# Loads run two units ahead in place of three from the tenth prepared unit on rather than from the twelfth

## The chip, the cores and the metric

One core of a Trainium2 chip. The metric is device time in microseconds (us) of one execution; medians over repeated executions are given with their range. "Clock" is the granted clock of TensorE: the share of its full rate that the throttle let through, 1.0 being all of it.

In the profile rows SPq is SyncE's queue, PE is TensorE, DVE VectorE and POOL GpSimd. A row gives start and duration in us, the line of kernel.py, the operation, what it writes and reads, and how many instructions are merged in it; a bracket gives the idle time before it and what ended it.

## The reference, cut to what matters

```python
B, H, S, D = 4, 8, 768, 64                # q, k, v in float32
for b in range(nb):                       # linear attention with decay, block by block
    intra = einsum(q_b, k_b) * Dmask;  intra = einsum(intra, v_b)
    inter = einsum(q_b * lam_pow, kv_state)
    out[b] = intra + inter
    kv_state = lam_block * kv_state + einsum(k_b * rev_pow, v_b)
x = out.transpose(0, 2, 1, 3).reshape(3072, 512)
return ((x @ w_a) * (x @ w_b)) @ w_out    # 512 -> 1536 -> 512
```

The kernel works on 24 units of 128 tokens (six for each of four batch entries). A unit needs its q, k and v, 256 KB each.

## The kernel before

Units are gathered into eight groups (4, 1, 2, 4, 4, 4, 4, 1) for the feed-forward product. While TensorE works on one group, the attention pieces of the next units are put between its matmuls at fixed slots. `used` counts prepared units; a load is put on SyncE's queue only if it is not too far ahead of it.

```python
LOOKAHEAD = (3, 2)
DMA_T_FROM = 9
...
PLAN = { ...
    2: [(0, "V", 6), (1, "T", 7), (1, "P", 8), (4, "T", 8), (4, "P", 9), (6, "S", 7),
        (6, "S", 8), (7, "V", 7), (6, "P", 10), (10, "V", 8),
        (12, "Q", (7, 8, 9, 10)), (12, "P", 11), (13, "V", 9), (14, "P", 12),
        (14, "O2", (9, 10))],
    3: [(3, "S", 11), (3, "S", 12)], ...
...
ld_pool = ctx.enter_context(tc.tile_pool(name="ld", bufs=4))   # per q, k and v
...
def load_x(w, u):
    ...
    nc.sync.dma_start(out=t, in_={"q": qr, "k": kr, "v": vr}[w][b, nb])
...
def pump():
    while pending:
        kind, c = pending[0]
        if kind in "abo":
            if len(staged) >= W_BUFS:
                return
        elif c >= used["u"] + LOOKAHEAD[used["u"] > 11]:
            return
        pending.pop(0)
        ...                                    # load_w or load_x
...
def prep_k(u):
    make_ks(u, "dve" if u < n0 + 2 else "pool")
    make_qs(u, "pool")
    used["u"] = u + 1
    if u >= DMA_T_FROM:                        # q and k transposed by a DMA, SBUF to SBUF
        qkT = qkT_pool.tile([128, 2, HP, 128], BF16, name="qkT", tag="qkT")
        nc.sync.dma_start_transpose(out=..., in_=U[u]["qk"]...)
...
def prep_v(u):
    make_vb(u, "pool" if u < n0 + 3 else "dve")
    pump()
...
def pieces_O(us, nxt=()):                      # "Q": outputs of us, scores of nxt
    kqs = [score_banks() for u in nxt]
    for u in us:
        inter(u)
    for u, kq in zip(nxt, kqs):
        scores(u, kq)                          # needs qkT of u
    for u in us:
        intra(u)
        ...
```

"P" of a unit is prep_k and then prep_v: scale k and q (GpSimd), put the transpose on SyncE's queue, cast v (VectorE), then pump the loads. So transposes and loads share one queue, in the order in which the program emits them. Below, L12 stands for unit 12's three loads and T10 for unit 10's transpose.

Of the kernel before, what the change touches and what calls it, by code (L numbers as in the profile page):

```python
# [30 lines left out]
LOOKAHEAD = (3, 2)  # L31
# [33 lines left out]
def kernel(  # L65
# [59 lines left out]
    def load_x(w, u):  # L125
        b, nb = divmod(u, NB)
        t = ld_pool.tile([128, H, D], F32, name=w + "f", tag=w + "f")
        nc.sync.dma_start(out=t, in_={"q": qr, "k": kr, "v": vr}[w][b, nb])
        raw[u, w] = t
# [10 lines left out]
    def load_w(kind, c):  # L140
        t = wst_pool.tile([128, 1024], F32, name="wst", tag="wst")
        if kind == "o":
            t = t[:].rearrange("p (k n) -> p k n", k=2)
            nc.sync.dma_start(out=t, in_=wo_r[:, 2 * c:2 * c + 2, :])
        else:
            w = W_CHUNKS[c]
            t = t[:, :KS * w].rearrange("p (k n) -> p k n", k=KS)
            r = wa_r if kind == "a" else wb_r
            nc.sync.dma_start(out=t, in_=r[:, :, w_off[c]:w_off[c + 1]])
        staged[kind, c] = t  # L150

    def cast_w(kind, c, eng):
        t = staged.pop((kind, c))
        if kind == "o":
            dst = wo_sb[:, 2 * c:2 * c + 2, :]
        else:
            dst = (wa_sb if kind == "a" else wb_sb)[:, :, w_off[c]:w_off[c + 1]]
        if eng == "act":
            nc.scalar.copy(dst, t)
        elif eng == "pool":  # L160
            nc.gpsimd.tensor_copy(dst[:, :, :128], t[:, :, :128])
            nc.gpsimd.tensor_copy(dst[:, :, 128:], t[:, :, 128:])  # L162
        else:
            nc.vector.tensor_copy(dst, t)
        pump()
# [9 lines left out]
    used = {"u": 0}  # L175
# [4 lines that stand above are left out]
            if kind in "abo":  # L180
                if len(staged) >= W_BUFS:
                    return
            elif c >= used["u"] + LOOKAHEAD[used["u"] > 11]:
                return
            pending.pop(0)
            if kind in "abo":
                load_w(kind, c)
            else:
                load_x(kind, c)
# [23 lines left out]
    for u in range(n0):  # L213
        load_x("v", u)
    pump()


# [69 lines left out]
# [3 lines that stand above are left out]
# [416 lines left out]
```

## Time and profile before

| | before |
|---|---|
| time, median (range) | 234.9 us (234.56 to 235.3, 5 runs) |
| profiled execution: time, span, granted clock | 235.62 us, 233.9 us, 1.0 |
| TensorE busy | 225.5 us (96%) |
| TensorE's waits behind the start-up | one, 1.49 us |
| TensorE asks for T10's result / has it | 77.56 / 79.05 us |

The profiled execution was a slow one, 0.7 us above the median and above all five runs quoted.

### The profile page before, as it was taken

Reading aid. Unit: us, or ns where it says so; the run is one execution under the profiler, and the core shown is the slowest. Engines: PE = TensorE matmul, PEld = TensorE weight load, DVE = VectorE, ACT = ScalarE, POOL = GpSimd, SP = SyncE. Lnnn points to the kernel's source line nnn. Section 1 sums busy time; section 2 is a strip of 40 time slices with the busy share of each in tenths; the row PEclk is TensorE's granted clock in tenths of the full one; section 3 lists DMA queues with packets and bytes.
Section 4 is the critical chain, followed back from the end, with each engine's and each line's share of the span. In section 5 each row is a group of like instructions: output and inputs, shape, how many; then the busy total and the mean of one; then the engine's idle time right before and its main releaser. Section 6 shows DMA issues by size and latency. Waiting matters only on the chain.

```text
span 233.9 us, 4520 instructions
## 1 busy us (share of the span) xinstructions
PE 225.5 (96%) x1775; PEld 124.7 (53%) x1775; DVE 118.3 (51%) x204; ACT 91.1 (39%) x172; POOL 50.6 (22%) x65
## 2 busy tenths in 40 slices
PE   7799999999999799999999999999999999999993
PEld 2474444459688454454544454544454544444493
DVE  0896557536579536775235574235583323332050
ACT  3585753066363243342243342333332333332261
POOL 6070000237463333553000543001200000000000
PEclk9999999999999999999999999999999999999999
DMA  4999999999999999998659997229300220000311
GB/s 154 301 286 350 349 366 288 295 191 224 198 229 174 207 220 203 213 193 162 234 198 215 211 178 134 90 90 207 67 3 0 90 92 0 1 0 23 114 45 48
DMA packets 96389, 38.84 MB, mean 166 GB/s; under 512 B 83312, under 2 KB 91888, under 8 KB 96368
## 3 DMA queue, kind: packets, MB, share of 16 engines
q1 hardware_dynamic: 96224, 38.54, 73.3%
q8 instruction: 14, 0.23, 0.4%
q14 instruction: 7, 0.06, 0.1%
q10 hardware_dynamic: 144, 0.00, 0.0%
HBM read 28.32 MB, written 6.29 MB: 148 GB/s over the span
## 4 chain that ended last, share of the span: by engine, by line
PE 90%; DMA 5%; ACT 1%; SPq 1%; issue 0%; DVE 0%
PE a_ps L435 27%; PE b_ps L435 26%; PE op L467 26%; DMA k<-in_k_dram 3%; PE o_ps L352 3%; PE kq L310 2%; DMA qkT<-qk 2%; PE o_ps L342 2%; PE kvd L366 1%; PE tps L296 1%; ACT o_kept L458 1%; SPq L209 1%; PE kq L578 1%; ACT xT L359 0%; PE kv L366 0%; PE tk L542 0%
## 5 line engine op out<-in xcount | busy, mean ns | idle before, releaser
L447 DVE TENSOR_TENSOR ab<-a_sb,b_ps 128x512 bf16<-128x512 bf16 (+2 forms) x96 | 52.5, 553 | 76.7 <-PE b_ps L435 56.7
L435 PE MATMUL a_ps<-xT,wa_sb 128*128 128x512 bf16 (+2 forms) x384 | 77.2, 326 | 0.6 <-ACT xT L359 0.6
L435 PE MATMUL b_ps<-xT,wb_sb 128*128 128x512 bf16 (+2 forms) x384 | 77.3, 326 | 0.0
L442 ACT CAST a_sb<-a_ps 128x512 bf16<-128x512 f32 (+2 forms) x96 | 45.6, 481 | 63.2 <-PE a_ps L435 61.6
L467 PE MATMUL op<-wo_sb,ab 128*128 128x512 bf16 (+2 forms) x312 | 65.6, 363 | 0.0
L435 PEld LDWEIGHTS <-wb_sb 128*128 128x128 bf16 x384 | 34.5, 98 | 28.6
L435 PEld LDWEIGHTS <-wa_sb 128*128 128x128 bf16 x384 | 33.7, 98 | 29.0 <-POOL wa_sb L162 0.6
L467 PEld LDWEIGHTS <-ab 128*128 128x128 bf16 x312 | 28.8, 98 | 29.9
L327 DVE TENSOR_TENSOR m<-kq,lotri 128x512 bf16<-128x512 f32 x47 | 29.4, 684 | 19.3 <-PE kq L310 19.0
L259 POOL TENSOR_TENSOR qk<-kf,lp_k 128x512 bf16<-128x512 f32 x18 | 19.0, 1057 | 76.4 <-DMA kf<-in_k_dram 69.8
L264 POOL TENSOR_TENSOR qk<-qf,lp_q 128x512 bf16<-128x512 f32 x20 | 21.7, 1087 | 23.4 <-DMA qf<-in_q_dram 23.4
L462 ACT COPY o_sb<-op 128x512 f32<-128x512 f32 (+2 forms) x19 | 10.3, 541 | 34.0 <-PE op L467 34.0
L359 ACT CAST xT<-o_ps 128x512 bf16<-128x512 f32 x22 | 12.0, 590 | 19.6 <-PE o_ps L352 19.2
L398 DVE TENSOR_TENSOR st<-kvd,bdiag 128x512 bf16<-128x512 f32 x18 | 12.3, 685 | 4.7 <-PE kvd L366 3.6
L273 DVE CAST vb<-vf 128x512 bf16<-128x512 f32 x17 | 11.3, 667 | 0.0
L298 ACT COPY qkT<-tps 128x1024 bf16<-128x1024 bf16 x5 | 5.1, 1012 | 9.9 <-PE tps L296 9.9
L197 PE MATMUL idle<-idle_sb 128*128 128x128 bf16 (+1 forms) x31 | 7.5, 384 | 1.3 <-DVE idle_sb L192 1.3
L310 PE MATMUL kq<-qkT 64*128 64x128 bf16 x160 | 6.7, 218 | 1.5 <-DMA qkT<-qk 1.5
L352 PE MATMUL o_ps<-m,vb 128*64 128x128 bf16 x192 | 7.9, 222 | 0.0
L273 POOL CAST vb<-vf 128x512 bf16<-128x512 f32 x7 | 4.7, 674 | 13.9 <-DMA vf<-in_v_dram 13.9
L342 PEld LDWEIGHTS <-st 128*128 128x128 bf16 x80 | 5.4, 98 | 2.8
L352 PEld LDWEIGHTS <-vb 128*64 128x64 bf16 x192 | 5.8, 109 | 1.4
(57 smaller groups left out, 87.4 us busy)
## 6 DMA issues: line engine op xcount, KB each, us to landing
vf<-in_v_dram SPq DMA_DIRECT2D x24, 256.0 KB, 5.1
qf<-in_q_dram SPq DMA_DIRECT2D x20, 256.0 KB, 4.5
kf<-in_k_dram SPq DMA_DIRECT2D x20, 256.0 KB, 4.8
out_dram<-o_sb SPq DMA_DIRECT2D x16, 256.0 KB, 2.0
wst<-in_moe_w_a_dram SPq DMA_DIRECT2D x6, 512.0 KB, 8.7
wst<-in_moe_w_b_dram SPq DMA_DIRECT2D x6, 512.0 KB, 8.8
wst<-in_moe_w_out_dram SPq DMA_DIRECT2D x6, 512.0 KB, 8.5
out_dram<-o_kept SPq DMA_DIRECT2D x7, 256.0 KB, 2.5
```

The source lines that it names most:

```text
L259: eng_of(eng).tensor_mul(qk[:, 1], raw.pop((u, "k")), lp_k[:, u % NB].to_broadcast([128, H, D]))
L264: eng_of(eng).tensor_mul(U[u]["qk"][:, 0], raw.pop((u, "q")), lp_q[:, u % NB].to_broadcast([128, H, D]))
L273: eng_of(eng).tensor_copy(vb, vf)
L310: nc.tensor.matmul(kq[i][:, hp, :], lhsT=d["kT"][p, hp, :], rhs=d["qT"][p, hp, :], start=True, stop=True, skip_group_check=True)
L327: nc.vector.tensor_mul(m, kq[i], lotri_bc)
L352: nc.tensor.matmul(d["o"][p, hp, :], lhsT=d["vb"][:, 2 * hp + i, :], rhs=d["m"](i, hp), start=(first and hp == 0), stop=True, skip_group_c ...
L359: nc.scalar.copy(xT[:, :, col:col + BLK], o_ps)
L398: nc.vector.tensor_mul(st[:].rearrange("p hp i d -> p hp (i d)"), ps[:].rearrange("p hp i d -> p hp (i d)"), bdiag_bc)
L435: nc.tensor.matmul(ps[:, :gt], lhsT=w_sb[:, s, f * 128:(f + 1) * 128], rhs=xT[:, s, :gt], start=(s == 0), stop=(s == KS - 1))
L442: nc.scalar.copy(a_sb[:, :gt], ps[:, :gt])
L447: nc.vector.tensor_mul(ab[:, f, :gt], a_sb[:, :gt], ps[:, :gt])
L467: nc.tensor.matmul(op[:, lo:hi], lhsT=ab[:, f, t * 128:(t + 1) * 128], rhs=wo_sb[:, f, lo:hi], start=(f == 0), stop=(f == FC - 1))
```

## The change

Its intent is to change from which unit on the loads run only two units ahead. One threshold moves:

```diff
-            elif c >= used["u"] + LOOKAHEAD[used["u"] > 11]:
+            elif c >= used["u"] + LOOKAHEAD[used["u"] > 9]:
```

## The prediction

> **What bounds the kernel now.** I first read the page's busy shares and the chain that ended last. TensorE is busy 96% of the span and the chain is nine tenths matmul, so time can only come out of TensorE's few gaps, or be lost by opening new ones.
>
> ```profile
> PE 225.5 (96%) x1775; PEld 124.7 (53%) x1775; DVE 118.3 (51%) x204; ACT 91.1 (39%) x172; POOL 50.6 (22%) x65
> PE 90%; DMA 5%; ACT 1%; SPq 1%; issue 0%; DVE 0%
> ```
>
> The DMA's 5% is what a change of loads could touch. Read in order of time, the chain has two DMA pieces: the first K load (7.92 us, at the start, not touched) and one transposing DMA in the middle. The second table of waits, TensorE's alone from 62.6 us to 231 us, has a single row: waited for, total us, times, longest.
>
> ```profile
> PE kq L310 <- DMA qkT<-qk: 1.5, 1, 1.5
> ```
>
> After 85 us the same view is empty. So the only TensorE wait behind the start-up is this one. The timeline of TensorE shows where it lies, in the third group (units 7 and 8):
>
> ```profile
> 77.16 0.40 PE L310 MATMUL kq<-qkT 64*128 64x128 bf16 x8
> 79.05 0.40 PE L310 MATMUL kq<-qkT 64*128 64x128 bf16 x8 [1.49 <-DMA qkT<-qk]
> 79.38 0.64 PE L352 MATMUL o_ps<-m,vb 128*64 128x128 bf16 x16
> ```
>
> By the plan this is slot 12, "Q" of units 7, 8, 9, 10: the first eight matmuls are the scores of unit 9, the second eight those of unit 10. Unit 10's transposed q and k are late. The chain in order of time says how late:
>
> ```profile
> 73.98 0.02 SPq L282
> ...
> 74.12 4.89 DMA qkT<-qk
> 79.01 0.05 issue
> 79.05 0.40 PE kq L310 x8
> ```
>
> Issued at 74.12, landed at 79.01. To find why it was issued so late I put the two engines that precede it side by side: SyncE's queue (first fence) and GpSimd (second). Transposes start at unit 9, so the one at 68.06 is unit 9's, the one at 74.12 unit 10's; between them are the three loads of unit 12, after them those of unit 13.
>
> ```profile
> 66.64 1.25 SPq L128 DMA_DIRECT2D vf<-in_v_dram  x1
> 68.06 2.21 SPq L282 DMA_TRANSPOSE qkT<-qk  x1
> 70.33 0.56 SPq L128 DMA_DIRECT2D qf<-in_q_dram  x1
> 70.94 1.66 SPq L128 DMA_DIRECT2D kf<-in_k_dram  x1
> 72.71 0.83 SPq L128 DMA_DIRECT2D vf<-in_v_dram  x1
> 74.12 1.86 SPq L282 DMA_TRANSPOSE qkT<-qk  x1
> 76.04 0.57 SPq L128 DMA_DIRECT2D qf<-in_q_dram  x1
> 76.67 1.07 SPq L128 DMA_DIRECT2D kf<-in_k_dram  x1
> 77.83 0.86 SPq L128 DMA_DIRECT2D vf<-in_v_dram  x1
> 78.81 3.70 SPq L282 DMA_TRANSPOSE qkT<-qk  x2
> ```
> ```profile
> 67.12 1.04 POOL L259 TENSOR_TENSOR qk<-kf,lp_k 128x512 bf16<-128x512 f32 x1 [1.28 <-DMA kf<-in_k_dram]
> 68.12 1.04 POOL L264 TENSOR_TENSOR qk<-qf,lp_q 128x512 bf16<-128x512 f32 x1
> 70.70 1.04 POOL L259 TENSOR_TENSOR qk<-kf,lp_k 128x512 bf16<-128x512 f32 x1 [1.54 <-PE kq L310]
> ```
>
> GpSimd scales K of units 0 to 3 not at all and of 4 and 5 not (VectorE does), so counting its L259 rows from unit 6 the pair at 67.12 and 68.12 is unit 10. Its data were ready at 68.12 + 1.04 = 69.16; the transpose went out at 74.12, 4.96 us later. In that time SyncE was issuing: unit 9's transpose until 70.27, then unit 12's loads until 73.54. One queue issues in program order, so the loads of unit 12 stand in front of the transpose that TensorE needs next.
>
> **What the Trainium skill says.** "Perfetto Trace Analysis", section "What 'DMA-bound' means", names an issuing sequencer whose track is solid DMA slices as a bound of its own; that is SyncE here from 66.64 on. The same page, "Per-instruction lifecycle", section "DMA Instruction — HWDGE", has the profiled slice begin when semaphores are satisfied and end when descriptors are generated, the movement itself not being in it. The trace agrees: slices last 0.56 to 2.21 us in the fence above, while loads land a median 4.5 to 5.1 us after issue and transposes 4.2 us (3.0 to 5.9). "DMA: Bandwidth & Descriptors", section "Issuing engines are not separate DMA queues", has all DMAs share the same 16 engines, so removing loads from in front of a transpose also removes their traffic: the mean DMA share from 70.00 to 77.56 us is 1.42, over full by overlapping packets.
>
> **The change part by part.** No operation is added or removed; instruction counts should be equal. Loads of a unit c go out while c < used + lookahead, after prep(u) has set used = u + 1 and put unit u's transpose on the queue. Before: after prep 9, used = 10, lookahead 3: unit 12; after prep 10: unit 13; after prep 11, lookahead 2, 12 + 2 = 14: nothing; after prep 12: unit 14. Changed: after prep 9, 10 + 2 = 12: nothing; after prep 10: unit 12; after prep 11: unit 13; after prep 12: unit 14. So exactly two triples move on the queue, each behind one transpose more:
> before T9, L12, T10, L13, T11, T12, L14; changed T9, T10, L12, T11, L13, T12, L14. All from L14 on is in the same order.
>
> Step 1, T10. It waits for GpSimd (69.16) and for SyncE to finish T9 (70.27), so it goes out near 70.3 instead of 74.1, 3.8 us earlier. With the 4.89 us it took, it lands near 75.2; with the slowest of all, 5.9, at 76.2. TensorE asks for it at 79.05 - 1.49 = 77.56. The wait of 1.49 us goes, with 1.4 to 2.4 us to spare.
>
> Step 2, L12 and T11. L12 follows T10: 70.3 + 1.9 = 72.2, against 70.33, so 1.9 us later, ending near 75.4. T11's data were ready at 70.70 + 2.04 = 72.74, so T11 at about 75.5 (before 78.81).
>
> Step 3, L13. From about 77.5 against 76.04, 1.5 later.
>
> Step 4, T12. Unit 12's K was issued at 70.94 and used by GpSimd from 76.48, 5.54 later; now 72.9 + 5.5 = 78.4, plus two GpSimd ops (2.04) = 80.5. Before, T12 was the second of the pair at 78.81, at 81.27. About 0.8 us earlier despite the later load, since L13 no longer holds up T11.
>
> Step 5, T13, T14. L14 near 81.8 (before 82.56). Unit 13's K, 77.5 + 0.6 + 5 = 83, plus 2.04 = 85.1 (T13 was at 85.94). T14 was at 90.45; near 89.7 now. The scores of 11 and 12 come at 92.32, those of 13 and 14 at 100.11; after a gain of 1.5 us at 90.8 and 98.6. T12 lands by 80.5 + 5.9 = 86.4, T14 by 95.6. Both in time.
>
> Step 6, VectorE. It casts V in program order, so a late V would hold up what follows. Unit 12's V now goes out near 74.3 (before 72.71); with the median 5.1 us it is there at 79.4. VectorE reached that cast at 82.29 and would reach it near 81.2.
>
> Step 7, what gives some back. Behind the wait, VectorE has unit 9's and 10's masks (four of 0.68 us), a cast of 0.42 and unit 9's state (0.69), which unit 10's first output matmuls need. Before, masks were broken by 0.60 us of waiting; now they run through from 77.59 to about 80.2, the cast to 80.6, the state to 81.3. TensorE wants it at 82.78 - 1.49 + 0.2 = 81.5. Level, with the casts on this engine ranging from 0.42 to 1.20 us: I take off 0 to 0.5 us, 0.15 in the mean.
>
> Sum: 1.49 - 0.15 = about 1.35 us of 233.9, all of it passed on, since no wait for anything follows up to the end. 234.9 - 1.35 = 233.55, say 233.6 us.
>
> **Rivals.**
> - *T10 is not held by the loads.* The chain puts a TensorE matmul (a_ps, ending 73.94) ahead of T10's semaphore instruction, and 0.58 us pass between 73.54 and 74.12. If that were a true dependency, T10 would stay and the time be 234.9. Against it: that matmul is at slot 10 or so, and T10 is emitted at slot 6; a DMA cannot wait for a later instruction of the program. The buffer it overwrites was last read by unit 6's scores, before 62 us. I take the name for a coincidence of two events (1 in 15).
> - *The wait only moves* to unit 9's state, or to PSUM banks whose masks are read later relative to TensorE: a gain of 0.5 to 1.0, so 234.0 to 234.4 (1 in 6).
> - *The shorter lookahead starves units 12 and 13.* For it: GpSimd already sits 3.74 us waiting for unit 12's K and 3.10 for unit 13's. Against: at 5.5 us per load the chain above still leads the need by 3 to 4 us, and VectorE's V cast by 1.8. A slow landing (the V loads reach 8.6 us) would cost TensorE 1 to 2 us: 235 to 236 (1 in 20).
>
> **Range and chances.** Full gain 233.2 to 233.8 with the before's scatter of about 0.3 either way; moved wait up to 234.4; null 234.9. Hence 232.9 to 234.6 for 8 in 10. Two per cent is 4.7 us, three times the only wait in reach; nothing of that size is in the trace in either direction, so within 2% has 0.97.
>
> **What would show it.** Right: SyncE's queue shows two transposes in a row near 68 and 70.3; the 1.49 us row is gone; the third group's end and all behind it lie about 1.4 us earlier; counts are equal. Step 1 is wrong if unit 10's transpose still starts near 74 or lands after 77.6; steps 4 to 6 are wrong if a new TensorE wait stands before the scores at 92 or 100, or VectorE waits on a V load near 81; step 7 is mis-sized if a wait above 0.3 us appears before the output matmuls near 81.3.

## The result, and the profile after

| | before | after |
|---|---|---|
| time, median (range), 5 runs each | 234.9 us (234.56 to 235.3) | 233.39 us (233.35 to 233.56) |
| profiled execution: time, span | 235.62, 233.9 us | 233.49, 231.8 us |
| TensorE's waits from 62 to 231 us | 1.49 us | none listed |
| instructions | 4520 | 4520 |

The ratio is 0.9938, with a 95% interval of 0.9923 to 0.9952: 0.6% faster, within 2%.

SyncE's queue after the change, in order of time (start, duration, line, what); "x2" is two transposes in a row:

```profile
68.19 4.64 SPq L282 DMA_TRANSPOSE qkT<-qk  x2
72.88 0.58 SPq L128 DMA_DIRECT2D qf<-in_q_dram  x1
73.91 0.37 SPq L128 DMA_DIRECT2D kf<-in_k_dram  x1
74.40 0.52 SPq L128 DMA_DIRECT2D vf<-in_v_dram  x1
75.03 2.55 SPq L282 DMA_TRANSPOSE qkT<-qk  x1
77.63 0.57 SPq L128 DMA_DIRECT2D qf<-in_q_dram  x1
...
80.19 2.01 SPq L282 DMA_TRANSPOSE qkT<-qk  x1
```

T9 and T10 now go out back to back; the second starts at 70.6 and lands 4.3 us later, at 74.9, where it was 74.12 and 79.01. L12 follows at 72.88, T11 at 75.03, L13 at 77.63, T12 at 80.19.

TensorE at the place of the wait, after the change (the number behind x is the matmuls in the row):

```profile
77.18 0.62 PE L310 MATMUL kq<-qkT 64*128 64x128 bf16 x16
77.73 0.64 PE L352 MATMUL o_ps<-m,vb 128*64 128x128 bf16 x16
...
83.66 1.03 PE L435 MATMUL a_ps<-xT,wa_sb 128*128 128x512 bf16 x4
```

The two rows of eight score matmuls with a gap have become one row of sixteen. The row that answers to the last one, in the kernel before:

```profile
85.31 1.03 PE L435 MATMUL a_ps<-xT,wa_sb 128*128 128x512 bf16 x4
```

From the L352 row to that one it is 5.93 us in both kernels (79.38 to 85.31, 77.73 to 83.66), so nothing was given back on the way. VectorE behind the scores, after the change:

```profile
77.61 2.48 DVE L327 TENSOR_TENSOR m<-kq,lotri 128x512 bf16<-128x512 f32 x4 [1.50 <-PE kq L310]
80.01 0.43 DVE L273 CAST vb<-vf 128x512 bf16<-128x512 f32 x1
80.37 0.68 DVE L398 TENSOR_TENSOR st<-kvd,bdiag 128x512 bf16<-128x512 f32 x1
80.97 0.41 DVE L273 CAST vb<-vf 128x512 bf16<-128x512 f32 x1
```

The four masks run through, unit 9's state is done at 81.05, and unit 12's v cast at 80.97 waits for nothing, although its load was moved back.

The profiled span shrank by 2.1 us, TensorE's work by 1.65; the other 0.45 us lie behind the last matmul, where storing the last tiles took 3.1 us in place of 3.6. The change doesn't touch that part, and the medians, with 1.5 us, don't show it; I count it as scatter of the profiled pair, whose first kernel was caught in a slow execution.

### The profile page after: what moved, and what is told of

It reads as the page before. It is cut to its first block, busy times and chain, and to the rows that moved or that the text cites. A ratio compares the mean times of both kernels' runs of the same rounds, so it can differ in the third digit from the quotient of the medians.

```text
span 231.8 us, 4520 instructions
## 1 busy us (share of the span) xinstructions
PE 225.2 (97%) x1775; PEld 124.6 (54%) x1775; DVE 115.9 (50%) x204; ACT 91.1 (39%) x172; POOL 50.6 (22%) x65
## 3 DMA queue, kind: packets, MB, share of 16 engines
q1 hardware_dynamic: 96224, 38.54, 72.9%
## 4 chain that ended last, share of the span: by engine, by line
PE 92%; DMA 3%; ACT 2%; SPq 1%; DVE 0%; issue 0%
PE a_ps L435 27%; PE b_ps L435 27%; PE op L467 27%; DMA k<-in_k_dram 3%; PE o_ps L352 3%; PE kq L310 2%; PE o_ps L342 2%; PE kvd L366 2%; PE tps L296 1%; ACT o_kept L458 1%; SPq L209 1%; PE kq L578 1%; ACT xT L359 0%; PE kv L366 0%; PE tk L542 0%; DVE scratch L531 0%
## 5 line engine op out<-in xcount | busy, mean ns | idle before, releaser
L273 DVE CAST vb<-vf 128x512 bf16<-128x512 f32 x17 | 9.4, 553 | 0.0
L352 PE MATMUL o_ps<-m,vb 128*64 128x128 bf16 x192 | 7.9, 222 | 0.0
L352 PEld LDWEIGHTS <-vb 128*64 128x64 bf16 x192 | 5.8, 109 | 1.4
```

Source lines behind the costliest of these rows:

```text
L273: eng_of(eng).tensor_copy(vb, vf)
L352: nc.tensor.matmul(d["o"][p, hp, :], lhsT=d["vb"][:, 2 * hp + i, :], rhs=d["m"](i, hp), start=(first and hp == 0), stop=True, skip_group_c ...
```

## The experiments

My theory: what counts is only how long SyncE's queue is held between T10's data being ready and T10's issue. Rivals: the shorter lookahead as such; the later loads of unit 13; a dependency of T10 on something else. The kernels e1 to e4 ran on one chip, e5 to after_again on a second, e8 and e4_again on a third and e9 on a fourth, each time beside runs of the kernel before (medians 234.75, 234.91, 234.95 and 235.12 us).

| kernel | queue around T10 | time, median (range) | ratio to before (95%) |
|---|---|---|---|
| before | T9 L12 T10 L13 T11 T12 | 234.75 (234.31 to 235.43) | |
| e1_l12_only | T9 T10 L12 L13 T11 T12 | 233.58 (233.36 to 234.19) | 0.9953 (0.9936 to 0.9970) |
| e2_l13_only | T9 L12 T10 T11 L13 T12 | 234.54 (234.17 to 235.05) | 0.9991 (0.9974 to 1.0008) |
| e3_qk12_front | T9 q12 k12 T10 v12 L13 T11 T12 | 233.67 (233.36 to 234.21) | 0.9957 (0.9940 to 0.9974) |
| e4_l12_l13_front | T9 L12 L13 T10 T11 T12 | 240.34 (239.61 to 241.72) | 1.0240 (1.0215 to 1.0264) |
| e5_l12_wide_rows | as before, L12 in 2 KB rows | 233.60 (233.52 to 233.75) | 0.9933 (0.9898 to 0.9969) |
| e6_three_ahead | T9 L12 T10 L13 T11 L14 T12 | 235.02 (234.33 to 237.66) | 1.0007 (0.9953 to 1.0062) |
| e7_two_ahead | T9 L11 T10 L12 T11 L13 T12 | 233.51 (233.36 to 234.11) | 0.9934 (0.9897 to 0.9970) |
| after_again | T9 T10 L12 T11 L13 T12 | 233.54 (233.35 to 233.78) | 0.9930 (0.9895 to 0.9966) |
| e8_front_kept_busy | as e4, 15 times 8 matmuls in the wait | 240.49 (239.41 to 241.23) | 1.0226 (1.0200 to 1.0252) |
| e4_again | as e4 | 239.76 (239.02 to 240.78) | 1.0211 (1.0190 to 1.0232) |
| e9_front_no_idle | as e4, 30 times 8 matmuls | 240.69 (240.12 to 241.24) | 1.0245 (1.0216 to 1.0273) |

**Half of the change: L12 alone.**

```diff
-            elif c >= used["u"] + LOOKAHEAD[used["u"] > 11]:
+            elif c >= used["u"] + LOOKAHEAD[used["u"] == 10 or used["u"] > 11]:
```

> Only unit 12's loads move behind unit 10's transpose; unit 13's loads stay in front of unit 11's (queue: T9 T10 L12 L13 T11 T12 L14). Queue-order theory: T10 is issued near 70.6 us and lands near 75, TensorE's wait for it is gone, and the time is that of the whole change, 233.4 us (233.2 to 233.7). Rival, half the gain is from unit 13's loads and T11: 234.1 or so. Rival, the gain is from the shorter lookahead as such: nearer 234.9.

Measured 233.58 us. Its profile shows T9 and T10 in a row, T10 issued at 70.2 and landed 4.2 us later, and no wait for a transpose. Four of six runs lie at 233.36 to 233.60, as the whole change; two lie at 234.12 and 234.19, and no trace of those two shows why.

**The other half: L13 alone.**

```diff
+            elif c >= used["u"] + LOOKAHEAD[used["u"] > 10]:
```

> The other half alone: unit 12's loads stay in front of unit 10's transpose, unit 13's move behind unit 11's (T9 L12 T10 T11 L13 T12 L14). Queue-order theory: T10 stays at 74.1 us, the wait of 1.49 us stays, 234.9 us (234.6 to 235.2). Rival, the moved traffic of unit 13 is worth something: 234.1.

Measured 234.54 us, not told apart from before (the interval holds 1). TensorE's waits from 62 us on, first row:

```profile
PE kq L310 <- DMA qkT<-qk: 0.8, 1, 0.8
```

The wait is there, smaller than in the trace of before: T10 was issued at 74.37, even later than 74.12, but landed 4.0 us later in place of 4.9. So the wait's size follows the landing. Why it was shorter is open: in the traces of before and of e6 L13 stands behind T10 and the landing took 4.9 us in both, here T11 stands there and it took 4.0. One trace doesn't part that from scatter, and the interval leaves room for up to 0.6 us from L13.

**Two of three loads in front.**

```diff
+            elif c >= used["u"] + LOOKAHEAD[used["u"] > 11 or (used["u"] == 10 and kind == "v")]:
```

> Two of unit 12's three loads (q and k) stay in front of unit 10's transpose, v goes behind it. Queue-order theory: T10 goes out when k's issue ends in the kernel before, 72.6 us, lands 4.3 to 4.9 us later, 76.9 to 77.5, just before TensorE asks at 77.56: wait 0 to 0.2 us, 233.4 to 233.6 us. A theory in which each load in front costs its share: two thirds of the loss stay, 234.4 us.

Measured 233.67 us: nearly the whole gain comes from taking one load of three out of the way. T10 was issued at 72.71 (expected 72.6) and landed 4.2 us later, at 76.9, before TensorE asked, and TensorE shows no wait for it. The cost is not a share per load: it begins when the landing passes the moment of need. (The trace is that of the fastest run; three of the six lie at 233.79 to 234.21, without a trace.)

**The cost doubled.**

```diff
+            elif c >= used["u"] + (4 if used["u"] == 10 else LOOKAHEAD[used["u"] > 11]):
```

> The suspected cost doubled: unit 12's and unit 13's loads both in front of unit 10's transpose (T9 L12 L13 T10 T11 T12 L14). Queue-order theory: T10 goes out a further triple later, some 3.3 us (70.33 to 73.54 took 3.2 in the kernel before), near 77.4, lands near 82; TensorE's wait grows from 1.49 to about 4.6 us and the time to 238.0 us (237.3 to 238.7). Rival, T10 is held by something else (a matmul): 234.9 us.

Measured 240.34 us: the direction was right, the size not, by 2.3 us. T10 was issued at 77.27 (expected 77.4) and TensorE waited 4.2 us (expected 4.6), so those steps hold. The rest lies behind the wait. TensorE:

```profile
77.28 0.40 PE L310 MATMUL kq<-qkT 64*128 64x128 bf16 x8
81.83 0.61 PE L310 MATMUL kq<-qkT 64*128 64x128 bf16 x8 [4.16 <-DMA qkT<-qk]
82.37 1.06 PE L352 MATMUL o_ps<-m,vb 128*64 128x128 bf16 x16
...
90.44 1.02 PE L435 MATMUL a_ps<-xT,wa_sb 128*128 128x512 bf16 x3
```

Eight score matmuls take 0.61 us against 0.40, sixteen output matmuls 1.06 against 0.64, and from L352 to the next group's first `a_ps` matmul it is 8.07 us against 5.93. The stretch 77.5 to 84 us of this kernel, by engine (busy us and instructions of TensorE, its weight loads, VectorE, ScalarE, GpSimd; then granted clock, DMA share, GB/s):

```profile
77.50:84.00 6.50, 2.34 (x34) 1.45 (x27) 2.81 (x5) 0.95 (x2) 2.37 (x3) 0.70 1.18 197
```

The granted clock is 0.70 there and 0.76 from 84 to 90 us; in the kernels before and after it is 1.00 in both stretches. Over the whole span the six runs had a clock of 0.984 to 0.993.

**The cost of L12 cut without a move** (relative error 0.30). Its output is wrong, which doesn't matter for the time.

```diff
+        if u == 12:
+            wide = {"q": q, "k": k, "v": v}[w][b].rearrange("h (a r) d -> (h a) (r d)", r=8)
+            nc.sync.dma_start(out=t[:].rearrange("p h d -> p (h d)"), in_=wide[0:128])
+        else:
+            nc.sync.dma_start(out=t, in_={"q": qr, "k": kr, "v": vr}[w][b, nb])
```

> The order of the kernel before, but unit 12's three loads read 128 rows of 2 KB in place of 1024 pieces of 256 bytes (the same 256 KB each; the wrong values, so a wrong result on purpose). If what matters is the time that unit 12's loads hold the queue, not their place as such: a 256 KB store in rows of 2 KB took 0.33 to 0.45 us to issue, so the three take about 1.3 in place of 3.2 us, T10 goes out near 71.8, lands near 76.5, no wait: 233.4 us (233.2 to 233.7). If the place in the order or the number of loads ahead is what matters: 234.9 us.

Measured 233.60 us, the whole gain, in the old order and with the old lookahead. SyncE's queue from unit 12's k load on:

```profile
70.56 1.24 SPq L130 DMA_DIRECT2D kf<-in_k_dram  x1
71.92 0.37 SPq L130 DMA_DIRECT2D vf<-in_v_dram  x1
72.86 1.26 SPq L286 DMA_TRANSPOSE qkT<-qk  x1
```

T10 goes out at 72.86, a microsecond later than expected, since the k load still took 1.24 us and 0.6 us passed before the transpose; it was enough. So neither the place in the order nor the number of units ahead matters by itself; what L12 costs in front of T10 does. How much of that is the queue and how much the movement, this run doesn't part, as the wide rows change both: against the trace of before T10 went out 1.26 us earlier and also landed 4.1 us after its issue in place of 4.9.

**Three ahead all the way, and two ahead all the way.**

```diff
-LOOKAHEAD = (3, 2)
+LOOKAHEAD = (3, 3)      # e6;   (2, 2) in e7
```

> Three units ahead all the way. Queue-order theory: T10 has unit 12's loads in front of it as before, so the wait of 1.49 us stays; T12 to T14 get a triple more in front of them, T14 near 94.6 and landing near 99 against a need at 100: 234.9 us (234.6 to 235.4). If a longer lookahead hurts by itself at every unit: 236 or more.

Measured 235.02 us, as before within the scatter; TensorE's one wait behind the start-up is T10's, 1.4 us. One run took 237.66 us at a mean clock of 0.993, as one of the kernel before did on the same chip (237.56, 0.993).

> Two units ahead all the way. Before unit 9 the queue has no transposes, so only unit 11's loads change place, to behind unit 9's transpose (T9 L11 T10 L12 T11 L13 T12). T9 goes out near 65.9, T10 behind unit 11's loads near 71.5, landing near 76.0 against a need at 77.2 to 77.6: no wait, 233.4 us (233.2 to 233.8), the same as the change. If two ahead starves GpSimd and the V casts: above 234.

Measured 233.51 us, as the change; T10 went out at 69.41, two microseconds before the 71.5 expected. But the profiled run, the slowest of six (234.11 us), has a new wait. TensorE, VectorE and GpSimd in that trace:

```profile
75.10 0.38 PE L366 MATMUL kvd<-vb,qk 128*128 128x128 bf16 x4 [0.74 <-DVE st L398]
```
```profile
72.82 1.30 DVE L273 CAST vb<-vf 128x512 bf16<-128x512 f32 x1
```
```profile
72.79 1.04 POOL L264 TENSOR_TENSOR qk<-qf,lp_q 128x512 bf16<-128x512 f32 x1
```

A cast that took 0.42 us elsewhere took 1.30 here. GpSimd had started its multiplication 0.03 us earlier, and the cast ended 0.29 us after that one. "SBUF — State Buffer" of the Trainium skill, section "Who interferes with whom", says that a VectorE cast in a two-port mode and a GpSimd instruction exclude each other from a shared pair of ports, the one that comes second blocking until the first is done. These rows agree in that the cast outlasted the multiplication; 0.29 us behind it is less than a whole cast, and no view shows which mode the cast ran in. Moving a load moves GpSimd's work against VectorE's, and here the two met; unit 7's state came 0.88 us later than in the trace of before (74.37 against 73.49), and TensorE lost 0.74 us. The profiled runs of the changed kernel show no such wait.

> The changed kernel again, beside the others of this call on the same chip: 233.4 us (233.2 to 233.7).

Measured 233.54 us, as expected.

**What the doubled cost's extra 2.3 us are.** TensorE repeats unit 9's scores in the wait (same values over the same ones; the result is right):

```diff
         for u, kq in zip(nxt, kqs):
+            if u == 10:
+                for _ in range(15):             # 30 in e9
+                    scores(nxt[0], kqs[0])
             scores(u, kq)
```

> The doubled cost once more (unit 12's and 13's loads in front of unit 10's transpose), but TensorE isn't idle in the wait: it repeats unit 9's scores 15 times (120 matmuls of some 35 ns apart, 4.1 us; the same values over the same ones, so the result is right). If the 2.3 us that the doubled cost came out above its expectation are the lower granted clock behind the long idle time (0.70 from 77.5 to 84 us, 0.76 from 84 to 90), the clock stays near 1.00 and the time is the changed kernel's plus the 4.4 us that the second half of the scores comes later: 237.8 us (237.3 to 238.3). If those 2.3 us are a cost of the order of the loads further on: 240.3 us, as without the filling.

> The doubled cost again, unfilled, beside the filled one on the same chip: 240.3 us (239.6 to 241), clock of the whole span near 0.986.

The unfilled kernel came out at 239.76 us, its clock at 0.993 in three runs and 0.986 in two. The filled one missed its expectation: 240.49 us. The filling ended at 81.0 us as meant, but T10 landed only 6.1 us after its issue, so that a hole of 2.43 us was left:

```profile
83.42 0.54 PE L310 MATMUL kq<-qkT 64*128 64x128 bf16 x8 [2.43 <-DMA qkT<-qk]
83.89 1.07 PE L352 MATMUL o_ps<-m,vb 128*64 128x128 bf16 x16
...
91.25 1.03 PE L438 MATMUL a_ps<-xT,wa_sb 128*128 128x512 bf16 x4
```

After it the matmuls are slow again, 7.36 us from L352 to the `a_ps` matmul, and the clock (the third number from the end, 84 to 90 us) is 0.75:

```profile
84.00:90.00 6.00, 6.00 (x65) 3.50 (x66) 2.64 (x5) 1.95 (x4) 1.56 (x2) 0.75 1.15 216
```

Three of the six runs had a clock of 0.993 and took 241.0 to 241.2 us; the other three, at 0.997 to 1.0, took 239.4 to 240.0. That speaks for the clock, but as a test of idle time it failed. Why the transpose landed later is not settled; the trace shows one instruction fetch in that stretch, where those of e4 show none. So the same once more with a filling that surely reaches over the landing:

> As the filled one, with 30 repeats in place of 15 (240 matmuls more, some 29 ns apart as that run showed, 7.0 us), so that the filling ends, near 84.5 us, after unit 10's transpose has landed even where that takes 6.1 us, and TensorE has no idle time there at all. If idle time is what lowers the granted clock: clock 0.997 or more in every run, the way from unit 10's scores to the next group's first a matmul takes 6.2 us as in the changed kernel (7.6 to 8.6 with the doubled cost, unfilled), and the time is the changed kernel's plus the 7.0 us that those scores come later, 240.5 us (240.0 to 241.0) with a narrow spread. If the clock falls for another reason: below 0.995 in some runs, and 242 us or more in those.

```profile
77.20 7.64 PE L310 MATMUL kq<-qkT 64*128 64x128 bf16 x256
84.77 0.64 PE L352 MATMUL o_ps<-m,vb 128*64 128x128 bf16 x16
...
90.70 1.03 PE L438 MATMUL a_ps<-xT,wa_sb 128*128 128x512 bf16 x4
```
```profile
77.50:84.00 6.50, 6.39 (x229) 6.22 (x225) 0.00 (x0) 0.00 (x0) 2.92 (x3) 1.00 1.34 190
```

Measured 240.69 us (expected 240.5), the clock 0.998 to 1.0 in all five runs. From L352 to the `a_ps` matmul it is 5.93 us, as in the kernels before and after, with T10 even later than in e4. So the loads further on are not the cause: with no idle time the slow stretch is gone. The extra cost of e4 was the lower clock behind a long wait, 2.14 us in its trace (8.07 - 5.93) and 1.13 in the repeated one (82.21 to 89.27 is 7.06).

## Why the prediction was right

**Step 1 (T10)** held: issued at 70.6 (70.3 predicted), landed at 74.9 (75.2), the wait gone. Halving the change (e1 against e2) and leaving the order alone while shortening L12 (e5) show that this step is the gain, to within the scatter of these runs. Not shown is how much of T10's earlier landing is the freed queue and how much the thinner traffic beside it: T10 took 4.3 us to land in place of 4.9.

**Steps 2 to 5 (the queue behind it)** held within 0.7 us each: L12 at 72.88 (72.2), T11 at 75.03 (75.5), L13 at 77.63 (77.5), T12 at 80.19 (80.5), T13 at 85.75 (85.1), T14 at 90.33 (89.7). None is late for TensorE. Part of the closeness is luck, since errors cancelled: L12 went out 0.7 us late but held the queue 2.0 us in place of 3.2, and unit 12's K went out at 73.91 (72.9) but reached GpSimd 4.2 us later, at 78.12 (78.4), in place of 5.5.

**Step 6 (VectorE's v cast)** held: reached at 80.97 (81.2), without a wait. (With the spacing of L12 in the kernel before, 2.38 us from its first load to its third, the v load comes out at 74.6, not 74.3; it went out at 74.40.)

**Step 7 (what is given back)** was too large by its 0.15 us: the state was done at 81.05 (81.3), before TensorE's output matmuls at 81.12. It had counted the masks at 0.68 us each; four in a row took 2.48. The kind of thing it feared, a cast stretched by GpSimd, did happen in the trace of e7, at another cast.

**The sum.** Two terms were a little off on the same side. The wait counts 1.49 us from the modelled end of the first eight score matmuls, but TensorE came out 1.65 us earlier: with data ready, the second eight start before the first have ended. With nothing given back, the gain was 1.5 us by the medians where 1.35 was predicted; 233.39 us against 233.6, inside the range. Here too is some luck: 1.49 us is the wait in an execution of 235.62 us; the trace of e2, a run of 234.61 us, has 0.8. What the median execution of the kernel before waits is not known.

**The rivals.** A dependency of T10 on a matmul is out: the transpose moved with the queue, at 70.6 in one kernel and 77.3 in another, and in e3 and e5 it went out at 72.71 and 72.86, before the matmul in question had ended (73.94 in the trace of before). The 0.58 us of nothing in front of T10 stayed in those two traces (0.57 us), and what it is stays open. Starved units are out for the change. The moved wait did not come in the changed kernel.

One thing that the prediction didn't say: the scatter shrank. Eleven runs of the changed kernel span 0.43 us (233.35 to 233.78); 41 of the 42 runs of the kernel before beside the experiments span 1.5 (234.19 to 235.69), and the other took 237.56 at clock 0.993. That fits a landing time that TensorE sees directly before and doesn't see after, and that can also cost clock when it is long; as no trace of those single runs exists, this is argued, not shown, and e1, whose trace has no such wait either, spans 0.83.

## What to carry to other kernels

When loads and a transfer that is needed soon share one queue, read how long the queue is held between the transfer's data being ready and its issue: a prefetch that is early enough for itself can still be too early for what stands behind it. Compare the landing with the moment of need, not load by load: here the cost was nothing up to that moment and nearly one for one after it (in e4 T10 landed 2.8 us later than before and the wait grew by 2.7), and a long wait on TensorE cost its clock besides (waits of 2.4 us and more did, one of 1.5 did not).

## What the Trainium skill lacked or had wrong

- "TensorE: Matmul & The Clock Gate", section "What's actually happening", puts the fall of the clock behind an idle window of about 3.4 us. Here a hole of 1.49 us left it at 1.00, and the stretches 77.5 to 84 us with holes of 4.2 and 4.1 us had a mean of 0.70 and 0.79, which agrees; but a hole of 2.43 us, behind 3.75 us of dense small matmuls, was followed by 0.75 from 84 to 90 us. The small matmuls alone were not the cause: 7.64 us of them without a hole stayed at 1.00.
- "DMA: Bandwidth & Descriptors", section "Issuing engines are not separate DMA queues", calls the sequencer's time to start a DMA usually small against the DMA. For one load in pieces of 256 bytes that was so (0.56 to 1.66 us against a median of 4.5 to 5.1 to landing), but three of them in a row held the queue 3.2 us in the kernel before (2.0 in the one after), long enough to make TensorE wait for what stood behind them.
- The same page gives a bandwidth for DMA transposes, but not the time from issue to landing beside loads: in the kernel before a median of 4.2 us, 3.0 to 5.9, for 128 by 1024 in bf16.
- No page says that a wait counted from the modelled end of pipelined matmuls comes out short: 1.49 us counted, 1.65 us gained.
